# A gated linear recurrence and a maxout layer on one core: stores, tiled TensorE work and the order of the weight loads

## The chip, the cores and the metric

The kernel runs on one core of a Trainium2 chip. The core has five engines with queues of their own: TensorE (PE, with its weight loads shown as PEld), VectorE (DVE), ScalarE (ACT), GpSimd (POOL) and SyncE (SP). SP issues all transfers between device memory and the on-chip memory here. The metric is the device time of one execution in microseconds (us); the figure given is the median of five runs.

## What is computed

The input is a gated linear recurrence over 768 steps for 4 batches and 8 heads of width 48, followed by a layer with two weight matrices, a maximum and an output matrix:

```python
for t in range(S):
    state = alpha[:, :, t, :, None] * state + einsum('bhd,bhe->bhde', k[:, :, t], v[:, :, t])
    y[:, :, t] = einsum('bhd,bhde->bhe', q[:, :, t], state)
x = y.transpose(0, 2, 1, 3).reshape(3072, 384)
h1 = x @ w1                      # 384 x 1024
h2 = x @ w2
out = maximum(h1, h2) @ w_out    # 1024 x 384
```

All inputs and the output are float32. The kernel multiplies in float16.

## The kernel before

The sequence is cut into 24 chunks of 128 steps, six per batch. The first six (batch 0) are worked as three "doubles" of 256 steps (`m` = 0, 1, 2), the other eighteen (`n` = 6 to 23) one by one. For a chunk, the logarithms of alpha are summed by a matmul (`p1`, tile `cs`; in a double `dcs`), exponentials of the sums scale k and q (`kt`, `qt`), both are transposed on TensorE (`p2`, tile `tp`; `dtp`), the scores are made (`p3`, tiles `pa` and `pb`; `dp`), DVE masks them into `pt` (two steps, `m0` and `m1`), and `p4` (tile `y`; `dy`) adds the scores' product with v and the carried state's share. ACT copies `y` into the columns of `xT` (`a3`). The state `w` passes from chunk to chunk through `kv`, `t32` and `T`.

The maximum is rewritten: max(h1, h2) = relu(x(w1 - w2)) + x w2. So `wd` holds w1 - w2 (made by DVE in two halves), `m16` holds w2 w_out (384 x 384, made once on TensorE: `prep_m`, in two halves `i` for each of three row groups `s`), and the output is relu(x wd) w_out + x m. Chunks that are ready are taken in blocks of up to three (384 columns): eight steps `fstep` (tile `h`), each followed by a relu into `g`, and then for each chunk `tstep` in two halves (tile `op`: three matmuls with `m`, three and five with `w_out`), an eviction into a buffer `outs` and a store.

The order of all this is not written out by hand. A small planner (`Sched`) runs when the program is built. Each `Op` has a guess of its duration on each engine that may do it (`engs`), operations it must wait for (`deps`), operations that must be planned ahead of it (`after`), on-chip buffers it takes and reads (`Ring`, `Buf`) and a priority. `pick` looks at all operations of an engine, computes the earliest start of each, and takes the one with the smallest pair (start, priority); the engine whose choice starts first is advanced. What is planned becomes the fixed order of each engine's queue; on the chip every instruction waits for its real inputs, and those behind it wait with it. A matmul that uses only part of the array (`p3`, `p4` and the doubles' like) is marked `tiled`; a tiled operation gets 0.5 off its priority while the planner's TensorE is in the tiled state, and a change of state is charged 0.09 us. The matmuls of the second layer have priorities of 1000 and more, and so fill what attention leaves. `refill` adds a block of them when few are pending, a block of fewer than three chunks only if TensorE would be idle.

PSUM is shared by three rings: `rx` (3 buffers) for `cs`, `tp`, `kv` and the like; `rp` (2) for `pa` and `pb`; `rm` (3) for `y`, `h`, `op` and the accumulators of `m`. The accumulator of one `s` is taken by its first half and given back after the copy that follows its second.

SP's queue holds, in the planned order, the loads of the first double in parts, the six halves of the weights, the loads of the other doubles, and then four loads per chunk (alpha, k, q, v) with the stores of finished chunks among them. The float32 weights lie in `w1f`, `w2f` and `wof`; once they are converted to float16 (`prep_wd`, `prep_w2`, the `woc` copies), their space is used for the chunks' loads. The order of the weight loads is the line

```python
for x in "d0 w20 w21 wo0 w10 wo1 w11 d1 d2".split():
```

where `d0` to `d2` are the doubles. There are `NO` = 4 buffers for `outs`; a store is an operation of SP with a priority of -1 that depends on its eviction.

Of the kernel before, what the change touches and what calls it, by code (L numbers as in the profile page):

```python
# [15 lines left out]
class Op:  # L16


    def __init__(self, sched, name, n, engs, fn, deps=(), lat=0.1, alloc=(), reads=(), prio=0.0, tiled=False, after=()):
        self.name, self.n, self.engs, self.fn, self.lat = name, n, engs, fn, lat  # L20
        self.deps, self.alloc, self.prio, self.tiled = [d for d in deps if d is not None], list(alloc), prio, tiled
        self.after = [d for d in after if d is not None]
        self.done = None
        for b in list(alloc) + list(reads):
            b.users.append(self)
        for e in engs:
            sched.todo[e].append(self)
# [22 lines left out]
class Sched:  # L50


    SEM = 0.06
    MARGIN = 0.25

    def __init__(self):
        self.todo = {e: [] for e in ("PE", "ACT", "DVE", "POOL", "SP")}
# [28 lines left out]
    def pick(self, e):  # L86
        now = self.free[e]
        best = None
        for op in self.todo[e]:
            t = self.start(op)  # L90
            if t is None:
                continue
            margin = self.MARGIN if e == "PE" and op.prio < 1000 else 0.0
            late = max(t + margin, now)
            key = (late, op.prio - (0.5 if op.tiled and self.tiled else 0.0))
            if best is None or key < best[0]:
                best = (key, max(t, now), op)
        return best

    def run(self):  # L100
# [37 lines left out]
def kernel(  # L138
# [23 lines left out]
    C = 128  # L162
    NCH = S // C
    NCG = B * NCH
# [151 lines left out]
    st = {n: {} for n in range(NCG)}  # L316
# [250 lines left out]
    def more(m, u):  # L567
        return u == 0 or m < ND - 1
# [85 lines left out]
    def copy(e, out, in_):  # L654
        {"ACT": nc.scalar.copy, "DVE": nc.vector.tensor_copy, "POOL": nc.gpsimd.tensor_copy}[e](out=out, in_=in_)  # L655
# [16 lines left out]
    def prep_te(e, f):  # L672
        copy(e, w2T[:, f : f + 2, :].rearrange("p i m -> p (i m)"),
             st["w2", f][:, 0:6, :].rearrange("p i m -> p (i m)"))
# [45 lines left out]
    def store(t0):  # L720
        nc.sync.dma_start(out=out[t0 : t0 + C, :], in_=outs[t0])


    NG, NO = 3, 4
    S = Sched()
    rx, rp, rm = Ring(3), Ring(2), Ring(3)
    rl = [Ring(6) for _ in range(4)]
# [5 lines left out]
    def op(*a, **k):  # L733
        return Op(S, *a, **k)
# [19 lines left out]
    prev = None  # L754
# [10 lines left out]
                    GD[m]["ld", i, x] = prev  # L765

    lw2, lw1, lwo = [None] * 2, [None] * 2, [None] * 2
    for x in "d0 w20 w21 wo0 w10 wo1 w11 d1 d2".split():
        if x[0] == "d":
            dloads_of(int(x[1]), 0.3 * int(x[1]))  # L770
        else:
            i = int(x[2])
            fn, to = {"w2": (load_w2, lw2), "wo": (load_wo, lwo), "w1": (load_w1, lw1)}[x[:2]]
            prev = to[i] = op(x, i, {"SP": WLOAD / 2}, lambda e, i=i, fn=fn: fn(i), lat=1.6, after=[prev], prio=0.5)
# [3 lines left out]
            for s, c in enumerate(({"ACT": 0.54}, {"DVE": 0.4}, {"POOL": 0.8}))] for i in range(2)]  # L778
    wdc = [[op("wd", i, {"DVE": 1.7}, lambda e, i=i: prep_wd(i), deps=[lw1[i], lw2[i]], prio=0.2)] for i in range(2)]
    woc = [op("woc", f, {"ACT": 0.75, "DVE": 0.55},  # L780
              lambda e, f=f: copy(e, wo16[:, f : f + 2, :], wof[:, f : f + 2, :]), deps=[lwo[f // 4]], prio=-0.3)
           for f in range(0, NF, 2)]
# [8 lines left out]
    w2t = []  # L791
    for f in range(0, NF, 2):
        b = Buf(rx)
        t = op("w2t", f, {"PE": 0.4}, lambda e, f=f: prep_t(f), lat=0.17, deps=w2c[f // NFH], alloc=[b], prio=f - 10)
        w2t.append(op("w2te", f, {"DVE": 0.6, "ACT": 0.75}, lambda e, f=f: prep_te(e, f), deps=[t], reads=[b], prio=-0.4))
    mdone = []
    for s in range(3):
        b = Buf(rm)
        prev = None
        for i in range(2):  # L800
            prev = op("m", s, {"PE": 0.66}, lambda e, s=s, i=i: prep_m(s, i), lat=0.17,
                      deps=w2t[2 * i : 2 * i + 2] + woc[2 * i : 2 * i + 2], after=[prev],
                      alloc=[b] if i == 0 else (), reads=[b] if i else (), prio=0.4 + 0.01 * s)
        mdone.append(op("mev", s, {"ACT": 0.4, "DVE": 0.45}, lambda e, s=s: copy(e, m16[:, s, :], mps[s]),
                        deps=[prev], reads=[b]))

# [10 lines left out]
    for m in range(ND):  # L817
        g = GD[m]
# [17 lines left out]
        for h in range(2):  # L836
# [3 lines left out]
                alloc=al("loga"), reads=[L[0]] + re("loga"))  # L840
            add("p1", h, {"PE": 0.5}, lambda e, m=m, h=h: dcs(m, h), [g["a1", h]], lat=0.17, alloc=[("cs", h)], reads=["loga"])
            add("en", h, {"ACT": 0.44}, lambda e, m=m, h=h: dexp(m, h, "en", -1.0), [g["p1", h]],
                alloc=al("en"), reads=[("cs", h)] + re("en"))
            add("ep", h, {"ACT": 0.44}, lambda e, m=m, h=h: dexp(m, h, "ep", 1.0), [g["p1", h]],
                alloc=al("ep"), reads=[("cs", h)] + re("ep"))
            add("gg", h, {"ACT": 0.2}, lambda e, m=m, h=h: dgg(m, h), [g["p1", h]],
                alloc=al("gg"), reads=[("cs", h)] + re("gg"))
            add("kt", h, {"POOL": 1.05}, lambda e, m=m, h=h: dqk(m, h, 1), [g["en", h], g["ld", 1, h]],
                alloc=al("kt"), reads=["en", L[1]] + re("kt"))
            add("qt", h, {"DVE": 0.9}, lambda e, m=m, h=h: dqk(m, h, 2), [g["ep", h], g["ld", 2, h]],  # L850
                alloc=al("qt"), reads=["ep", L[2]] + re("qt"))
            add("v", h, {"POOL": 0.95} if m else {"POOL": 0.95, "ACT": 0.6}, lambda e, m=m, h=h: dv(e, m, h), [g["ld", 3, h], sdv[m % 2]],
                alloc=al("v"), reads=[L[3]] + re("v"))
            add("p2", h, {"PE": 0.44}, lambda e, m=m, h=h: dtp(m, h), [g["qt", h], g["kt", h]], lat=0.17,
                alloc=[("tp", h)], reads=["qt", "kt"])
            add("v2", h, {"DVE": 0.66, "ACT": 0.95}, lambda e, m=m, h=h: dtpe(e, m, h), [g["p2", h]],
                alloc=[("qk", h)], reads=[("tp", h)])
            add("p3", h, {"PE": 0.36}, lambda e, m=m, h=h: dp(m, h), [g["v2", h]], lat=0.17,
                alloc=[("pa", h), ("pb", h)], reads=[("qk", h)], tiled=True)
            for t in range(2):  # L860
                add("m" + str(t), h, {"DVE": 0.66}, lambda e, m=m, h=h, t=t: dmask(m, h, t),
                    [g["p3", h], smask, g.get(("m0", h))],
                    alloc=[] if t else [("pt", h)], reads=[(("pa", "pb")[t], h)] + ([("pt", h)] if t else []))
        add("pk", 0, {"PE": 0.38}, lambda e, m=m: dkv(m), [g["kt", 1], g["v", 1]], lat=0.17,
            alloc=[("kv", u) for u in range(2) if more(m, u)], reads=["kt", "v"], tiled=True)
        for u in range(2):
            m1, u1 = dbefore(m, u)
            if m1 >= 0:
                Bp, gp = B2[m1], GD[m1]
                add("g", u, {"POOL": 0.25}, lambda e, m=m, u=u: dg(m, u), [gp["gg", 1], g["gg", 1]],  # L870
                    alloc=[("g", u)], reads=[Bp["gg"], "gg"])
                if more(m, u):
                    add("t32", u, {"POOL": 0.56}, lambda e, m=m, u=u: dt32(m, u), [g["g", u], gp["w", u1]],
                        alloc=[("t32", u)], reads=[("g", u), Bp["w", u1]])
                first = u == 0 or m == 0
                for t in range(2):
                    add(f"T{t}", u, {"POOL": 0.56}, lambda e, m=m, u=u, t=t: dT(m, u, t),
                        [g["g", u], gp["w", u1], sdv[m % 2], g.get(("T0", u)) if t else None],
                        alloc=["T"] if first and t == 0 else (),
                        reads=[("g", u), Bp["w", u1]] + ([] if first and t == 0 else ["T"]))  # L880
            if more(m, u):
                add("w", u, {"DVE": 0.35}, lambda e, m=m, u=u: dw(m, u), [g["pk", 0], g.get(("t32", u))],
                    alloc=[("w", u)], reads=[("kv", u)] + ([("t32", u)] if m1 >= 0 else []))
        add("p4", 0, {"PE": 1.1 if m else 0.85}, lambda e, m=m: dy(m), [g["m1", 1], g["v", 1], g["T1", 1]], lat=0.17,
            alloc=[("y", 0), ("y", 1)], reads=[("pt", 0), ("pt", 1), ("qk", 0), ("qk", 1), "v", "T"], tiled=True)
        for u in range(2):
            G[2 * m + u]["a3"] = add("a3", u, {"ACT": 0.5}, lambda e, m=m, u=u: dx(m, u), [g["p4", 0]], reads=[("y", u)])

# [2 lines left out]
    for n in range(2 * ND, NCG):  # L891
        c = n % NCH
        g = G[n]
# [27 lines left out]
        if c:  # L921
            pg = G[n - 1]
            add("g", {"POOL": 0.25}, lambda e, n=n: vg(n), [pg["gg"], g["gg"]], alloc=["g"], reads=[B_[n - 1]["gg"], "gg"])
            if c < NCH - 1:
                add("t32", {"POOL": 0.56}, lambda e, n=n: vt32(n), [g["g"], pg["w"]], alloc=["t32"],
                    reads=["g", B_[n - 1]["w"]])
            for t in range(2):
                add(f"T{t}", {"POOL": 0.56}, lambda e, n=n, t=t: vT(n, t), [g["g"], pg["w"]],
                    alloc=["T"] if t == 0 else (), reads=["g", B_[n - 1]["w"]] + (["T"] if t else []))
                if t:  # L930
                    g["T1"].after.append(g["T0"])
        if c < NCH - 1:
            add("kv", {"PE": 0.18}, lambda e, n=n: p3k(n), [g["kt"], g["v1"]], lat=0.17, alloc=["kv"], reads=["kt", "v"])
            add("w", {"DVE": 0.75}, lambda e, n=n: vw(n), [g["kv"], g.get("t32")], alloc=["w"],
                reads=["kv"] + (["t32"] if c else []))
        add("p4", {"PE": 0.42 if c else 0.25}, lambda e, n=n: p4(n), [g["m1"], g["v1"], g.get("T1")], lat=0.17,
            alloc=["y"], reads=["pt", "v", "qk"] + (["T"] if c else []), tiled=True)
# [6 lines left out]
    def refill(now, idle):  # L944
        while pend and pend[0].done is not None:
            pend.pop(0)
        if len([o for o in pend if o.done is None]) > 2 or nxt[0] >= NCG:
            return
        if wdc[0][0].done is None or wdc[0][0].done > now + 0.3:
            return  # L950
        a = nxt[0]
        k = 0
        while k < WMAX // C and a + k < NCG and G[a + k]["a3"].done is not None and G[a + k]["a3"].done <= now + 0.3:
            k += 1
        if k == 0 or (k < WMAX // C and not idle):
            return
        nxt[0] += k
        W, a0 = k * C, a * C
        bg = Buf(rg16)
        rel = []  # L960
        xs = [G[a + i]["a3"] for i in range(k)]
        for f in range(NF):
            bh = Buf(rm)
            o = op("f", a, {"PE": 3 * max(W / 2400 + 0.0025, 0.07)}, lambda e, a0=a0, W=W, f=f: fstep(a0, W, f),
                   lat=0.17, deps=xs + wdc[f // NFH], after=pend[-1:], alloc=[bh] + ([bg] if f == 0 else []), prio=1000 + a)
            pend.append(o)
            rel.append(op("relu", a, {"ACT": 0.08 + W / 1200, "DVE": 0.1 + W / 960},
                          lambda e, a0=a0, W=W, f=f: relu(e, a0, W, f), deps=[o], reads=[bh, bg], prio=n))
        for i in range(k):
            bo, bs = Buf(rm), Buf(ro)  # L970
            for half in range(2):
                o = op("t", a + i, {"PE": (0.98, 0.82)[half]}, lambda e, a0=a0, i=i, half=half: tstep(a0, i, half),
                       lat=0.17, deps=mdone + woc + (rel[:3] if half == 0 else rel), after=pend[-1:],
                       alloc=[bo] if half == 0 else (), reads=[bg] if half else [bg], prio=1000 + a)
                pend.append(o)
            ev = op("oev", a + i, {"ACT": 0.4, "DVE": 0.45}, lambda e, t=a0 + i * C: oevict(e, t), deps=[o],
                    alloc=[bs], reads=[bo], prio=n)
            op("st", a + i, {"SP": 0.55}, lambda e, t=a0 + i * C: store(t), lat=1.2, deps=[ev], reads=[bs], prio=-1)
        return True

    S.refill = refill
# [32 lines left out]
```

## Time and profile before

| what | us |
|---|---|
| five runs | 149.21, 147.67, 147.69, 148.96, 151.07 |
| their median | 148.96 |
| the profiled execution | 148.49 |
| its span, first to last instruction | 146.7 |
| TensorE's first matmul | 4.01 |
| transposes of the second double begin | 28.29 |
| last matmul begins to drain; last eviction starts | 143.24; 143.32 |

Busy time of the engines in stretches of the span (us; DMA is the mean busy share of the 16 DMA engines, and can pass 1 where transfers overlap an edge of the stretch):

| stretch | PE | DVE | ACT | POOL | DMA |
|---|---|---|---|---|---|
| 0 to 12 | 5.03 | 5.86 | 4.86 | 9.42 | 0.88 |
| 12 to 19.5 | 4.96 | 6.37 | 5.05 | 4.23 | 1.06 |
| 19.5 to 28.3 | 6.34 | 3.70 | 6.20 | 1.95 | 1.07 |
| 28.3 to 45 | 16.70 | 12.92 | 12.30 | 14.17 | 0.98 |
| 45 to 60 | 14.49 | 9.73 | 11.82 | 11.19 | 0.99 |
| 60 to 90 | 30.00 | 20.03 | 24.10 | 19.33 | 0.96 |
| 90 to 118 | 28.00 | 19.77 | 21.48 | 18.82 | 0.99 |
| 118 to 143.3 | 25.24 | 4.56 | 14.47 | 3.01 | 0.20 |

A busy TensorE is not one at its peak: the end of a matmul is modelled, so a small pause between two matmuls can be hidden in "busy". Such pauses are read from the distance between two starts. The granted TensorE clock is 0.998 of full speed over the span.

### The profile page before, as it was taken

How to read it: one execution, taken by the hardware profiler on the slowest of the kernel's cores; microseconds unless marked ns; L12 is line 12 of the kernel's file. 1: busy time of each engine (PE TensorE's matmuls, PEld its weight loads, DVE VectorE, ACT ScalarE, POOL GpSimd, SP SyncE). 2: the span in 40 equal slices, each digit the busy share in tenths (PEclk: the TensorE clock that was granted, in tenths of full speed). 3: DMA queues.
4: the chain of work that ended last, by engine and by line, in shares of the span. 5: the costliest groups of instructions: out<-in, count | busy, mean ns of one | idle time of the engine just before them, and what ended most of it. 6: DMA issues, size and time to landing. Idle time of an engine off the chain costs nothing.

```text
span 146.7 us, 4865 instructions
## 1 busy us (share of the span) xinstructions
PE 130.8 (89%) x1958; PEld 87.4 (60%) x1958; DVE 82.9 (57%) x161; ACT 100.8 (69%) x223; POOL 82.1 (56%) x184
## 2 busy tenths in 40 slices
PE   0375789599999998999999999999999999999990
PEld 0353646476877676666667666666666665656550
DVE  4647754578494793886457865587469693100000
ACT  4433876676787778778677976886778656925721
POOL 7987400768997869664188954848468871000000
PEclk9999999999999999999999999999999999999999
DMA  4999999999799899979999999989999951102012
GB/s 121 261 348 382 381 341 238 245 274 202 137 201 217 166 220 222 196 144 234 197 206 192 216 200 221 225 196 228 180 215 230 202 132 54 54 30 111 24 69 92
DMA packets 93542, 28.62 MB, mean 195 GB/s; under 512 B 87888, under 2 KB 91984, under 8 KB 93520
## 3 DMA queue, kind: packets, MB, share of 16 engines
q1 hardware_dynamic: 93520, 28.32, 81.8%
q8 instruction: 15, 0.25, 0.7%
q14 instruction: 7, 0.06, 0.1%
HBM read 23.59 MB, written 4.72 MB: 193 GB/s over the span
## 4 chain that ended last, share of the span: by engine, by line
PE 72%; SPq 12%; DMA 9%; ACT 2%; issue 1%; DVE 1%; POOL 1%; ACTq 0%; POOLq 0%; DVEq 0%
PE op L711 21%; PE h L694 20%; PE op L708 8%; SPq L203 7%; DMA dqf<-in_q_dram 6%; PE y L465 6%; SPq L223 4%; DMA w1f<-in_alpha_dram 3%; PE pa L406 3%; PE tp L388 3%; PE tp L390 2%; PE cs L330 2%; PE kv L417 2%; PE dtp L533 1%; SPq L233 1%
## 5 line engine op out<-in xcount | busy, mean ns | idle before, releaser
L711 PE MATMUL op<-wo,g 128*128 128x384 f16 x192 | 37.3, 326 | 0.0
L694 PE MATMUL h<-xT,wd 128*128 128x384 f16 (+1 forms) x216 | 36.6, 309 | 0.0
L701 ACT ACTIVATE g<-h 128x384 f16<-128x384 f32 (+1 forms) x53 | 23.7, 467 | 2.8 <-PE h L694 2.6
L694 PEld LDWEIGHTS <-wd 128*128 128x128 f16 x216 | 19.2, 98 | 9.2
L711 PEld LDWEIGHTS <-g 128*128 128x128 f16 x192 | 17.9, 98 | 11.3
L425 DVE TENSOR_TENSOR pt<-pa,u 128x512 f16<-128x512 f32 x18 | 12.4, 691 | 12.5 <-PE pb L406 6.9
L655 ACT COPY outs<-op 128x384 f32<-128x384 f32 x20 | 9.6, 479 | 14.0 <-PE op L711 14.0
L367 POOL TENSOR_TENSOR T<-w,g 48x192 f16<-48x192 f32 x30 | 15.6, 519 | 1.2
L655 ACT COPY qk<-tp 128x1024 f16<-128x1024 f16 x15 | 15.2, 1012 | 1.1 <-PE tp L390 1.0
L708 PE MATMUL op<-m,xT 128*128 128x384 f16 x72 | 15.6, 325 | 0.0
L425 DVE TENSOR_TENSOR pt<-pb,u 128x512 f16<-128x512 f32 x18 | 12.3, 683 | 0.1
L469 ACT CAST xT<-y 128x384 f16<-128x384 f32 x18 | 8.7, 484 | 4.6 <-PE y L465 4.3
L521 POOL TENSOR_TENSOR dkt<-dkf,den 128x384 f16<-128x384 f32 x6 | 6.2, 1048 | 9.6 <-ACT den L503 9.6
L352 POOL TENSOR_TENSOR kt<-wof,en 128x384 f16<-128x384 f32 x6 | 6.5, 1087 | 8.3 <-ACT en L340 7.9
L436 DVE TENSOR_TENSOR w<-kv,t 48x192 f32<-48x192 f32 x24 | 8.5, 353 | 3.8 <-PE kv L417 3.4
L340 ACT ACTIVATE en<-cs 128x384 f32<-128x384 f32 x18 | 9.0, 498 | 0.8 <-PE cs L334 0.8
L699 DVE TENSOR_SCALAR g<-h 128x256 f16<-128x256 f32 (+1 forms) x19 | 8.6, 475 | 1.6 <-PE h L694 1.5
L340 ACT ACTIVATE ep<-cs 128x384 f32<-128x384 f32 x18 | 9.0, 502 | 0.0
L465 PE MATMUL y<-pt,v 128*32 128x128 f16 x288 | 9.0, 220 | 0.0
L352 POOL TENSOR_TENSOR kt<-w1f,en 128x384 f16<-128x384 f32 x6 | 6.4, 1062 | 3.7 <-ACT en L340 1.8
L708 PEld LDWEIGHTS <-xT 128*128 128x128 f16 x72 | 6.4, 97 | 3.3
L352 POOL TENSOR_TENSOR kt<-w2f,en 128x384 f16<-128x384 f32 x6 | 6.0, 1001 | 3.7 <-ACT en L340 3.3
(121 smaller groups left out, 269.7 us busy)
## 6 DMA issues: line engine op xcount, KB each, us to landing
out_dram<-outs SPq DMA_DIRECT2D x24, 192.0 KB, 3.0
w2f<-in_moe_w_dram SPq DMA_DIRECT2D x2, 768.0 KB, 7.5
wof<-in_moe_w_out_dram SPq DMA_DIRECT2D x2, 768.0 KB, 10.6
w1f<-in_moe_w_dram SPq DMA_DIRECT2D x2, 768.0 KB, 11.9
dvf<-in_v_dram SPq DMA_DIRECT2D x3, 384.0 KB, 5.8
wof<-in_alpha_dram SPq DMA_DIRECT2D x6, 192.0 KB, 4.9
wof<-in_k_dram SPq DMA_DIRECT2D x6, 192.0 KB, 4.3
wof<-in_q_dram SPq DMA_DIRECT2D x6, 192.0 KB, 4.4
```

Of the source, the lines that this page charges most:

```text
L203: nc.sync.dma_start(out=dloads[m][i][:, hs], in_=src[0, hs, m * C2 : (m + 1) * C2, :].rearrange("h (p j) d -> p h (j d)", j=2),)
L340: nc.scalar.activation(out=t, in_=csv, func=ACTF.Exp, scale=scale)
L352: nc.gpsimd.tensor_mul(out=kts[n % NB][:, :, 0:D], in0=loads[n][1], in1=st[n]["en"])
L367: nc.gpsimd.tensor_mul(out=st[n]["T16"][ps, :, D * t : D * t + D], in0=st[n - 1]["w"][ps], in1=st[n]["g"][ps].unsqueeze(2).to_broadcast([D ...
L425: nc.vector.tensor_mul(out=s["pt"][:, t], in0=s["pp"][t], in1=ub)
L465: nc.tensor.matmul(y[o : o + 32, b // 4, :], lhsT=lhsT, rhs=rhs, start=start, stop=stop)
L469: nc.scalar.copy(out=xT[:, :, n * C : (n + 1) * C], in_=st[n]["y"])
L655: {"ACT": nc.scalar.copy, "DVE": nc.vector.tensor_copy, "POOL": nc.gpsimd.tensor_copy}[e](out=out, in_=in_)
L694: nc.tensor.matmul(h[:, 0:W], lhsT=wd16[:, s, f * 128 : (f + 1) * 128], rhs=xT[:, s, a : a + W], start=(s == 0), stop=(s == 2))
L701: nc.scalar.activation(out=gts[a][:, f, 0:W], in_=hs[a, f][:, 0:W], func=ACTF.Relu)
L708: nc.tensor.matmul(op, lhsT=xT[:, s, t0 : t0 + C], rhs=m16[:, s, :], start=(s == 0), stop=False)
L711: nc.tensor.matmul(op, lhsT=gts[a][:, f, i * C : (i + 1) * C], rhs=wo16[:, f, :], start=False, stop=(f == NF - 1))
```

## The change

There are four edits in the planner and its input; no instruction of the computation is added or removed.

- Stores: an `Op` can have a `slack`, which is added to its earliest start when SP chooses and when it is planned. All stores but those of the last four chunks get 3.0 us. `NO` goes from 4 to 6.
- Tiled work: `pick` counts the tiled operations that can start within 0.1 us. On TensorE, outside the tiled state and after 45 us of the plan, if fewer than two are ready, a tiled operation that has been ready for less than `HOLD` = 2.5 us gets 2000 added to its priority, so that ready full-array work goes first. Within the tiled state a tiled operation now gets 2.0 off, not 0.5.
- Weight loads: w1's second half is loaded before w_out's second half.
- `prep_m`: the first half of each accumulator must be planned after `p4` of the first double.

```diff
+    HOLD = 2.5
...
     def pick(self, e):
         now = self.free[e]
         best = None
-        for op in self.todo[e]:
-            t = self.start(op)
+        ready = [(op, self.start(op)) for op in self.todo[e]]
+
+        hold = e == "PE" and not self.tiled and sum(op.tiled for op, t in ready if t is not None and t <= now + 0.1) < 2
+        for op, t in ready:
             if t is None:
                 continue
             margin = self.MARGIN if e == "PE" and op.prio < 1000 else 0.0
-            late = max(t + margin, now)
-            key = (late, op.prio - (0.5 if op.tiled and self.tiled else 0.0))
+            late = max(t + margin + op.slack, now)
+            prio = op.prio
+            if op.tiled and self.tiled:
+                prio -= 2.0
+            elif op.tiled and hold and now - t < self.HOLD and now > 45.0:
+                prio += 2000.0
+            key = (late, prio)
             if best is None or key < best[0]:
-                best = (key, max(t, now), op)
+                best = (key, max(t + op.slack, now), op)
         return best
...
-    NG, NO = 3, 4
+    NG, NO = 3, 6
...
-    for x in "d0 w20 w21 wo0 w10 wo1 w11 d1 d2".split():
+    for x in "d0 w20 w21 wo0 w10 w11 wo1 d1 d2".split():
...
-    mdone = []
+    mdone, mfirst = [], []
     for s in range(3):
         b = Buf(rm)
         prev = None
         for i in range(2):
             prev = op("m", s, {"PE": 0.66}, lambda e, s=s, i=i: prep_m(s, i), lat=0.17,
-                      deps=w2t[2 * i : 2 * i + 2] + woc[2 * i : 2 * i + 2], after=[prev],
+                      deps=w2t[2 * i : 2 * i + 2] + woc[2 * i : 2 * i + 2], after=[prev] if i else [],
                       alloc=[b] if i == 0 else (), reads=[b] if i else (), prio=0.4 + 0.01 * s)
+            if i == 0:
+                mfirst.append(prev)
...
+        if m == 0:
+            for o in mfirst:
+                o.after.append(g["p4", 0])
...
-            op("st", a + i, {"SP": 0.55}, lambda e, t=a0 + i * C: store(t), lat=1.2, deps=[ev], reads=[bs], prio=-1)
+            op("st", a + i, {"SP": 0.55}, lambda e, t=a0 + i * C: store(t), lat=1.2, deps=[ev], reads=[bs], prio=-1, slack=3.0 if a + i < NCG - 4 else 0.0)
```

More of the change, by code (lines that the diff above doesn't have):

```diff
@@ L16, with __init__ @@
 class Op:
-    def __init__(self, sched, name, n, engs, fn, deps=(), lat=0.1, alloc=(), reads=(), prio=0.0, tiled=False, after=()):
+    def __init__(self, sched, name, n, engs, fn, deps=(), lat=0.1, alloc=(), reads=(), prio=0.0, tiled=False, after=(), slack=0.0):
         self.name, self.n, self.engs, self.fn, self.lat = name, n, engs, fn, lat
@@ L22, in __init__ @@
         self.after = [d for d in after if d is not None]
-        self.done = None
+        self.done, self.slack = None, slack
         for b in list(alloc) + list(reads):
```

## The prediction

> **What bounds the kernel now.** I read the page first: busy shares by engine, the slices, the chain that ended last. Then TensorE's waits in two stretches, its timeline around the places that the diff touches, and the busy time by stage.
>
> The page's lines (columns: busy us, share of the span, instructions; then tenths busy in 40 slices of 3.67 us; then the chain's shares by engine):
>
> ```profile
> PE 130.8 (89%) x1958; PEld 87.4 (60%) x1958; DVE 82.9 (57%) x161; ACT 100.8 (69%) x223; POOL 82.1 (56%) x184
> ...
> PE   0375789599999998999999999999999999999990
> ...
> DMA  4999999999799899979999999989999951102012
> ...
> PE 72%; SPq 12%; DMA 9%; ACT 2%; issue 1%; DVE 1%; POOL 1%; ACTq 0%; POOLq 0%; DVEq 0%
> ```
>
> PE is full from the eighth slice to the end, the DMA engines are full up to about 118 us. The waits of PE, first for 0 to 28.3 us, then for 28.3 to 143.3 us, say which of the two sets the end (columns: who waited for whom, us in total, times, longest):
>
> ```profile
> PE dcs L488 <- ACT dloga L478: 6.2, 3, 4.0
> PE dtp L533 <- DVE dqt L519: 1.7, 1, 1.7
> PE dpa L550 <- ACT dqk L655: 1.5, 1, 1.5
> PE wtp L669 <- DVE dw L591: 1.1, 1, 1.1
> PE dpa L550 <- DVE dqk L655: 0.8, 1, 0.8
> PE mp L683 <- ACT wo L655: 0.6, 1, 0.6
> ```
> ```profile
> PE dtp L533 <- DVE dqt L519: 1.7, 1, 1.7
> PE cs L330 <- ACT loga L325: 0.5, 1, 0.5
> ```
>
> After 28.29 us, in 115 us, PE waits once, for 0.5 us (the 1.7 us ends at 28.29). So the kernel is a head of 28.3 us in which loads and short dependences rule, 115 us of PE work without holes, and a tail of 3.4 us (last eviction and store). The time changes if the head gets shorter, if PE does more before 28.29, if its work takes fewer us, or if holes open.
>
> The head's end, from the PE timeline (start, us, engine, line, operation, count, idle before):
>
> ```profile
> 19.52 0.90 PE L683 MATMUL mp<-wo,w2T 128*128 128x384 f16 x4
> 21.02 3.41 PE L683 MATMUL mp<-wo,w2T 128*128 128x384 f16 x20 [0.59 <-ACT wo L655]
> ...
> 25.48 1.14 PE L694 MATMUL h<-xT,wd 128*128 128x256 f16 x9
> 28.29 0.40 PE L533 MATMUL dtp<-ident,dqt 128*128 128x128 f16 x4 [1.67 <-DVE dqt L519]
> ```
>
> The chain of waits shows what the dtp waits for:
>
> ```profile
> 18.28 8.86 DMA dqf<-in_q_dram
> ...
> 27.23 1.02 DVE dqt L519
> ...
> 28.29 0.62 PE dtp L533 x8
> ```
>
> The second double's q is issued at 18.28 and lands at 27.1, behind all six weight halves in one queue that is full.
>
> **Part 1: load order and m.** w1's second half and wo's second half (768 KB each) change places in SP's queue. From the DMA issues by window the fifth half (wo 1) is issued at 8.06 and lands 12.1 us later, at 20.2; the sixth (w1 1) at 9.45, 13.1 us later, at 22.5. So w1 1 will land at about 20.2 and wo 1 at 22.5. What is behind them, dq of the second double among it, has the same bytes ahead and keeps 27.1. Consequences, step by step:
> - The second subtraction for wd (DVE, 1.76 us) runs 20.2 to 22.0 instead of 22.6 to 24.3. Nobody waited for it; gain 0 by itself.
> - The conversion of wo 1 (ACT 0.83 us beside DVE 0.72 us or less) runs 22.5 to 23.3. The second halves of m (12 matmuls) cannot start before. The twelve of the first halves can: one s at 19.5, the other two when the copies of the first y free PSUM (ring of 3; about 20.3 and 20.8 by the 0.5 us copies). They are 4 x 0.165 us each, so PE is through with them at about 21.5 and waits 1.8 us, in place of 0.59 us. The second halves then run 23.3 to 25.3 against an end of 24.4 before. All three accumulators of the ring are held until then, so no h can fill that wait.
> - Behind the waiting m on PE: two dcs (0.86 us), nine h (1.0 us), then dtp. 25.3 + 0.86 + 1.0 = 27.2, still before 28.29: the 1.67 us hole there covers the 0.9 us lost. Without that cover it would cost 0.9 us. On ACT, den and dep of the second double start at about 25.8 and dep ends near 26.7, 0.5 us before q has landed; dkt on POOL (1.0 us) ends near 27.5, before its transposes at 28.5.
> - y of the first double before m: the trace has it there already (dy begins at 18.10, the first mp at 19.52). The new edge fixes that order. 0.
>
> Sum of part 1: 0; between -1.7 (the hole before 28.29 filled with h) and +0.7 us (every step 0.7 us later than I put it, cover spent).
>
> **Part 2: tiled work taken together.** A chunk has one p3 (8 matmuls, 48-row tiles) and one y (28 matmuls, 32-column tiles), between full-array work. The price of going in and out, from the PE timeline:
>
> ```profile
> 80.82 1.63 PE L694 MATMUL h<-xT,wd 128*128 128x384 f16 x9
> 82.38 0.23 PE L406 MATMUL pa<-qk 48*128 48x128 f16 x1
> ```
>
> Nine h take 1.56 us from first start to the p3, where nine h ahead of full-array work take 1.46 (77.88 to 79.34). The same 0.10 us shows as 0.58 against 0.49 for three h ahead of a y. The y at 93.41 is followed by cs 0.52 us later; the y at 62.53 is followed by a p3 0.51 us later. So a p3 put straight behind a y saves its entry, 0.10 us, and nothing of y's way out.
>
> The Trainium skill, page "TensorEngine Tiling (Array Packing)", section Tiling Modes (Key Properties), says that a change of tiling mode drains the array. y and p3 are different modes, so by that rule alone a pair drains between its two members and after them, as often as two single groups do less one: the rule speaks against most of the gain. The rows say that the drain after y is indeed there in the pair (0.51 to 0.52 us either way) but that the entry cost on the full-array side is saved. By the rule read strictly part 2 is worth 0, by the rows 0.10 us a pair. I take the rows.
>
> Pairs: between 45 us and the end I count 18 p3, 18 y and one dy in 30 groups, so seven pairs stand already. If each chunk made one group, 19 would remain, 11 x 0.10 = 1.1 us. The hold lasts 2.5 us at most and drops when no full-array work is ready, so I take eight new pairs: -0.8 us. Bounds 0 and -1.1; two y side by side (same mode, some 0.25 us each with the way out) could add a little, the scores of two chunks cannot stand together since pa and pb fill their ring of two.
>
> What the hold delays: a held p3 delays its two masks (DVE 0.69 + 0.68 us), and they free pa and pb for the next chunk's p3; a held y delays the xT copy (ACT 0.48 us) and the h of its block. Full-array work runs meanwhile. Cover: the last y ends at 129.42 and the last block's h starts at 133.82, so 3.9 us remain after the copy; at 58.4 to 63.4 us (third y of the first single block to its h) 4.5 us. Below these the delay costs 0, above one for one.
>
> **Part 3: stores with slack, six output buffers.** Twenty of 24 stores move back by 3 us in the plan, past the loads behind them. Between 38 and 117 us SP waited 13 us in store instructions (sum of its rows). But PE's only wait on a load in that time is the 0.5 us at 55.4:
>
> ```profile
> PE cs L330 <- ACT loga L325: 0.5, 1, 0.5
> ```
>
> It hangs on a load issued at 49.89 and landed 4.84 us later; two stores (1.56 and 0.64 us of issue at 40.2 and 42.3) stand ahead of it. With them behind, the hole may close: 0 to -0.5, I take -0.3. POOL's queue issues no DMA. Two more buffers keep evictions from waiting for the later stores: three outputs come 1.8 us apart at the fastest, then a pause; a store needs 0.48 + 3 + 3.6 us. The last four stores keep no slack, so the tail of 3.4 us stays.
>
> **Sum.** 0 - 0.8 - 0.3 = -1.1 us on the profiled execution's 148.49 us (146.7 span, 1.8 around it): 147.4. The median of the five runs is 148.96, 0.47 above that execution, so 147.9 us on the scale of the runs. About 1% (1.5 us) is what a measurement of this kernel tells from no change.
>
> **The rivals.**
> - *The head is used* (0.15). With wd complete at 22.0 and DVE free, more h go into PE's queue ahead of dtp, and the 1.67 us hole fills: five more steps of three 256-wide h at 0.33 us. Against it: the ring of three held by m, and relu on an ACT busy with den and dep. 147.9 - 1.5 = 146.4 us.
> - *The hold stretches the attention chain, slower than before* (0.25). p3 of a chunk needs pa and pb back from the chunk before, so a hold is passed from chunk to chunk. Place: 45 to 129 us. Price: each us by which the last y comes after about 133.3 us. It decides from 3.9 us in all, 0.22 us per chunk over 18. With 0.35 us per chunk the last y is 6.3 us later, 2.4 us past its cover, plus a like hole where the early stock of h and op is thin (near 55 us, where the one wait stands), less the 0.8 gained: about 151.0 us. For it: a tiled step may be held 2.5 us, ten times that mean. Against: a hold only lets ready work go first, and PE's total is unchanged.
> - *It does nothing* (0.14). Drains as the page has them, or few new pairs; the hole at 55 us moves: 148.9 us.
>
> The likeliest (0.46) is the sum, 146.9 to 148.7. Faster by over 1% (under 147.5): four tenths of that, 0.18, and the first rival, 0.15, and 0.01 of the third: 0.34. Slower by over 1% (over 150.4): 0.24 from the second. Within 1%: 0.42. The range goes from 146.0 to 150.4 us: it leaves out the stretched chain's larger part (0.16) and a full head with all pairs (0.04).
>
> **What would show it.** Part 1: mp in two runs of twelve, with a wait of about 1.8 us for wo, dtp still near 28.3. Part 2: some 22 tiled groups after 45 us, and TensorE from dtp to its last op shorter by about 1 us. Part 3: stores after loads in SP's list, no wait of cs for loga. I am wrong if dtp moves by over 0.7 us either way, if waits of PE after 28.3 us sum to over 1.5 us, or if the blocks of h have other widths than six of 384 and three of 256.

## The result, and the profile after

| | before | changed |
|---|---|---|
| median of all runs, us | 149.05 (79 runs) | 148.97 (44 runs) |
| lowest, us | 147.52 | 146.82 |
| ratio | | 0.997, 95% interval 0.9948 to 0.9992 |
| profiled execution, us (span) | 148.49 (146.7) | 149.74 (148.0) |

The change takes 0.3% off, some 0.4 us, where 1.1 us was forecast. The ratio compares the faster executions of the two kernels alone, since some executions of either are a per cent or more slower, and both profiled executions of the changed kernel (149.74 us here, 149.02 in run e5) are among the slower ones, so their holes are read beside those of e6, which has the same order on TensorE from 46 to 57 us and whose profile (148.03 us) is not. I read the trace for where the time goes, and the ratio for how much it is.

The page of the changed kernel, the lines that answer to those of before:

```profile
PE 130.4 (88%) x1958; PEld 88.6 (60%) x1958; DVE 87.4 (59%) x163; ACT 99.2 (67%) x221; POOL 83.1 (56%) x184
...
PE   0474896899999697999999999999999999999990
...
DMA  4999999999989597989998999999989742010212
```

A new dip stands in PE's row at the 14th to 16th slice (48 to 59 us), where before has nines and one 8, and the DMA row dips in the same slices. PE's waits from 28.3 us to the end say the same:

```profile
PE cs L338 <- ACT loga L333: 1.8, 2, 1.4
PE h L702 <- ACT xT L477: 0.5, 1, 0.5
PE tp L396 <- ACT qk L663: 0.2, 1, 0.2
```

Before had one wait of 0.5 us there. The changed kernel's sum to 2.57 us. What was gained is visible too. In the PE timeline of the changed kernel a chunk's y is followed by the next chunk's p3 and only then by full-array work (a few of the rows):

```profile
82.02 0.24 PE L342 MATMUL cs<-gcol,loga 128*128 128x2 f16 x4
82.19 0.24 PE L473 MATMUL y<-qk,T 112*32 112x128 f16 x4
...
82.71 0.23 PE L414 MATMUL pa<-qk 48*128 48x128 f16 x1
...
83.04 0.50 PE L702 MATMUL h<-xT,wd 128*128 128x384 f16 x2
```

Counted over the whole timeline from 45 us on, the 37 tiled steps stand in 19 groups; they stood in 30. And the head, from the same view:

```profile
19.49 2.52 PE L691 MATMUL mp<-wo,w2T 128*128 128x384 f16 x12
23.31 2.11 PE L691 MATMUL mp<-wo,w2T 128*128 128x384 f16 x12 [1.31 <-ACT wo L663]
...
26.12 1.14 PE L702 MATMUL h<-xT,wd 128*128 128x256 f16 x9
27.97 0.40 PE L541 MATMUL dtp<-ident,dqt 128*128 128x128 f16 x4 [0.70 <-DVE dqt L527]
```

The first and second halves of m are parted by a wait for wo, as worked out, and dtp begins at 27.97 (28.29 before).

How the largest hole is made is in PE's order. First the changed kernel, then the one before, at the same work (some rows of each):

```profile
49.59 0.82 PE L702 MATMUL h<-xT,wd 128*128 128x256 f16 x6
51.78 0.32 PE L338 MATMUL cs<-loga,cmat 128*128 128x384 f16 x1 [1.37 <-ACT loga L333]
51.94 0.24 PE L342 MATMUL cs<-gcol,loga 128*128 128x2 f16 x4
52.11 0.23 PE L414 MATMUL pa<-qk 48*128 48x128 f16 x1
...
52.44 0.41 PE L473 MATMUL y<-pt,v 128*32 128x128 f16 x16
```
```profile
50.25 0.49 PE L694 MATMUL h<-xT,wd 128*128 128x256 f16 x3
50.68 0.23 PE L406 MATMUL pa<-qk 48*128 48x128 f16 x1
...
51.28 0.41 PE L465 MATMUL y<-pt,v 128*32 128x128 f16 x16
...
52.08 0.33 PE L330 MATMUL cs<-loga,cmat 128*128 128x384 f16 x1
```

Before, p3, kv, y and tp stand ahead of the sums of chunk 9. The hold pushes p3 and y behind them, and the queue is in order: when chunk 9's alpha is late, p3 waits with it. The load of that alpha was not issued late: at 45.63, where before issued it at 45.87. It landed 5.5 us after its issue, against 4.1 us before, and behind it SP stood 2.81 us in the issue of the next load (SP's list of the changed kernel: start, us):

```profile
43.33 1.07 SPq L729 DMA_DIRECT2D out_dram<-outs  x1
44.44 0.43 SPq L202 DMA_DIRECT2D w2f<-in_v_dram  x1
44.97 0.62 SPq L729 DMA_DIRECT2D out_dram<-outs  x1
45.63 0.44 SPq L202 DMA_DIRECT2D w2f<-in_alpha_dram  x1
46.17 2.81 SPq L202 DMA_DIRECT2D w2f<-in_k_dram  x1
```

Two stores, moved back by the slack, now stand right ahead of it; before they stood ahead of chunk 8's alpha and k (40.17 and 42.31). That alone does not make it late: in the seven profiles of other kernels with the two stores in this place (e2, e4, e6, e7, e14 to e16) it landed after 4.0 to 5.1 us, and in the nine without them after 4.1 to 4.8. In e5 it took 5.8.

The wait of h for xT is a wait for a buffer, not for its numbers. This h is the last of the eight steps of the block of chunks 4 and 5, and the other seven had run. But h and y take their PSUM from one ring of three, and a buffer came free only when ACT had copied the y of chunk 7. ACT, in order too, stood at the logarithm of chunk 10's alpha, with that copy behind it (three rows of ACT, then PE's):

```profile
56.70 0.52 ACT L333 ACTIVATE loga<-w1f 128x384 f16<-128x384 f32 x1 [1.37 <-DMA w1f<-in_alpha_dram]
57.13 0.99 ACT L663 COPY qk<-tp 128x1024 f16<-128x1024 f16 x1
58.03 0.48 ACT L477 CAST xT<-y 128x384 f16<-128x384 f32 x1
```
```profile
58.56 0.49 PE L702 MATMUL h<-xT,wd 128*128 128x256 f16 x3 [0.53 <-ACT xT L477]
```

### The profile page after: what moved, and what is told of

It reads as the page before. It is cut to its first block, busy times and chain, and to the rows that moved or that the text cites. A ratio compares the mean times of both kernels' runs of the same rounds, so it can differ in the third digit from the quotient of the medians.

```text
span 148.0 us, 4866 instructions
## 1 busy us (share of the span) xinstructions
PE 130.4 (88%) x1958; PEld 88.6 (60%) x1958; DVE 87.4 (59%) x163; ACT 99.2 (67%) x221; POOL 83.1 (56%) x184
## 3 DMA queue, kind: packets, MB, share of 16 engines
q1 hardware_dynamic: 93520, 28.32, 80.3%
## 4 chain that ended last, share of the span: by engine, by line
PE 72%; DMA 12%; SPq 7%; ACT 3%; issue 2%; DVE 1%; POOL 1%; ACTq 0%
PE op L719 21%; PE h L702 20%; DMA wof<-in_moe_w_out_dram 8%; PE op L716 8%; PE y L473 5%; DMA w1f<-in_alpha_dram 4%; PE pa L414 3%; SPq L231 3%; SPq L211 2%; PE tp L396 2%; PE tp L398 2%; PE cs L338 2%; SPq L202 1%; PE kv L425 1%; PE mp L691 1%
## 5 line engine op out<-in xcount | busy, mean ns | idle before, releaser
L719 PE MATMUL op<-wo,g 128*128 128x384 f16 x192 | 36.8, 326 | 0.0
L663 ACT COPY outs<-op 128x384 f32<-128x384 f32 x21 | 10.1, 480 | 16.5 <-PE op L719 16.5
L663 ACT COPY qk<-tp 128x1024 f16<-128x1024 f16 x14 | 14.2, 1017 | 2.3 <-PE tp L398 2.2
L375 POOL TENSOR_TENSOR T<-w,g 48x192 f16<-48x192 f32 x30 | 15.1, 503 | 1.1
```

The lines of the kernel that those rows point to most:

```text
L375: nc.gpsimd.tensor_mul(out=st[n]["T16"][ps, :, D * t : D * t + D], in0=st[n - 1]["w"][ps], in1=st[n]["g"][ps].unsqueeze(2).to_broadcast([D ...
L719: nc.tensor.matmul(op, lhsT=gts[a][:, f, i * C : (i + 1) * C], rhs=wo16[:, f, :], start=False, stop=(f == NF - 1))
```

## The experiments

For the profiles I compare the stretch from the second double's dtp to the start of the last op group, PE's idle in it, and the number of tiled groups after 45 us, counted in the timeline. "Net" is the stretch less the idle. "Hole" is PE's idle from 45 to 60 us.

| kernel | groups | dtp | stretch | idle | net | hole | ratio (interval) |
|---|---|---|---|---|---|---|---|
| before | 30 | 28.29 | 109.43 | 0.51 | 108.92 | 0.51 | 1 |
| changed | 19 | 27.97 | 110.99 | 2.57 | 108.42 | 2.57 | 0.997 (0.9948-0.9992) |
| e5, changed again | 19 | 27.85 | 110.39 | 1.99 | 108.40 | 1.99 | 0.9963 (0.9929-0.9997) |
| e1, pairs alone | 20 | 28.34 | 108.65 | 0.53 | 108.12 | 0.00 | 0.9959 (0.9922-0.9995) |
| e11, e1 again | 20 | 28.77 | 108.23 | 0.29 | 107.94 | 0.18 | |
| e2, slack alone | 31 | 28.38 | 109.98 | 0.79 | 109.19 | 0.72 | 0.9988 (0.9958-1.0018) |
| e3, loads and m alone | 30 | 28.32 | 110.03 | 1.06 | 108.97 | 0.69 | 1.0021 (0.9986-1.0057) |
| e13, changed without slack | 20 | 28.40 | 109.55 | 1.11 | 108.44 | 0.38 | 0.999 (0.996-1.002) |
| e6, changed with old loads | 19 | 27.77 | 109.49 | 1.07 | 108.42 | 1.07 | 0.9958 (0.9931-0.9985) |
| e15, e6 again | 19 | 28.54 | 109.45 | 1.02 | 108.43 | 1.02 | |
| e4, changed, hold from 60 | 22 | 30.82 | 107.86 | 0.00 | 107.86 | 0.00 | 0.9971 (0.9938-1.0004) |
| e14, e4 again | 22 | 28.27 | 108.91 | 0.81 | 108.10 | 0.81 | |
| e7, e4 with old loads | 22 | 28.13 | 107.85 | 0.00 | 107.85 | 0.00 | 0.994 (0.9915-0.9965) |
| e16, e7 again | 22 | 28.34 | 108.72 | 0.70 | 108.02 | 0.70 | 0.9923 (0.9895-0.995) |
| e8, pairs from 60 alone | 22 | 27.61 | 109.46 | 1.42 | 108.04 | 1.42 | 0.9932 (0.9905-0.9958) |
| e12, e8 again | 22 | 28.25 | 107.87 | 0.00 | 107.87 | 0.00 | |
| e9, tiled steps apart | 37 | 28.32 | 109.92 | 0.34 | 109.58 | 0.34 | 1.0065 (1.0039-1.0091) |

### e1, e2, e3: one part alone

Each is the kernel before with one part of the change. The parts as diffs, shortened:

```diff
# e1
...
+            prio = op.prio
+            if op.tiled and self.tiled:
+                prio -= 2.0
+            elif op.tiled and hold and now - t < self.HOLD and now > 45.0:
+                prio += 2000.0
# e2
-    NG, NO = 3, 4
+    NG, NO = 3, 6
-            ... prio=-1)
+            ... prio=-1, slack=3.0 if a + i < NCG - 4 else 0.0)
# e3
-    for x in "d0 w20 w21 wo0 w10 wo1 w11 d1 d2".split():
+    for x in "d0 w20 w21 wo0 w10 w11 wo1 d1 d2".split():
...
+        if m == 0:
+            for o in mfirst:
+                o.after.append(g["p4", 0])
```

> The kernel before with the hold and the stronger pull of the tiled state alone; stores, buffers and load order as before. 20 tiled groups after the first p3 (30 before). Theory (the pairs save 0.10 us each, and the hold puts a cs whose alpha is late ahead of a ready p3 between 48 and 58 us): PE waits for loga there sum to 1 to 2.5 us, the ten pairs give back 1.0, ratio 0.995 to 1.008. Rival (the holes come from the moved stores and loads): no wait above 0.6 us after 28.3, ratio 0.992 to 0.994. Second rival (a change of tiling mode drains, so pairs save nothing): with the holes, ratio 1.005 to 1.015.

> The kernel before with the slack of the stores and six output buffers alone. 31 tiled groups. Theory: the order on PE up to 62 us is that of before, the one wait of cs stays between 0 and 0.6 us, ratio 0.997 to 1.002. Rival (moved stores make the holes): PE waits after 28.3 sum to over 1.5 us, ratio 1.006 to 1.015.

> The kernel before with w1's second half loaded ahead of w_out's second half, and m after the first double's y, alone. 30 tiled groups. Theory: mp waits 1.0 to 1.9 us for wo, dtp of the second double starts at 28.0 to 28.5 as before, ratio 0.997 to 1.003. Rival (the late m moves dtp): dtp at 28.8 or later, ratio over 1.003. Rival (the holes after 45 us come from this part): PE waits after 28.3 sum to over 1.5 us.

Pairs alone: 0.9959, with 20 groups and none of the large holes: in its trace PE waits for loga only 0.2 us after dtp. Of the two readings that I had put up, the ratio fits the first (0.995 to 1.008) and the waits fit its rival, so the early hold alone is not what makes the holes. Slack alone: 0.9988, nothing that can be measured. Loads and m alone: 1.0021, with dtp where it was (28.32) and mp waiting 1.7 us. In these profiles no single part makes a hole of 1 us or more.

### e4, e14, e7: the hold from 60 us on, with the new and the old load order

```diff
-            elif op.tiled and hold and now - t < self.HOLD and now > 45.0:
+            elif op.tiled and hold and now - t < self.HOLD and now > 60.0:
```

e7 has the load order and the place of m of before besides.

> The changed kernel with the hold from 60 us of the plan on, not from 45: 22 tiled groups, and the order of TensorE up to about 62 us is that of before. Theory: the waits of PE between 45 and 60 us fall back to under 0.7 us, eight pairs stay at 0.10 us each, ratio to before 0.990 to 0.996. Rival (pairs save nothing): ratio 0.998 to 1.002. Rival (the holes come from stores or loads): waits of 1.5 to 2.5 us between 45 and 60 us as in the changed kernel, ratio about 1.00 or more.

> Run e4 once more. If the late head belongs to the program: mp waits about 3 us for wo, a slice of PEclk near 22 us at half, dtp of the second double after 30 us. If it is chance of the execution: mp waits 1.3 to 2 us, PEclk full, dtp at 27.8 to 28.4.

In e4's profile the waits between 45 and 60 us are gone and the stretch is 1.57 us shorter than before's, yet the ratio of its executions is 0.9971 and not 0.990 to 0.996. What the profile lost, it lost in the head: dtp begins at 30.82. The PE timeline of e4:

```profile
19.43 2.24 PE L691 MATMUL mp<-wo,w2T 128*128 128x384 f16 x12
24.80 3.17 PE L691 MATMUL mp<-wo,w2T 128*128 128x384 f16 x12 [3.13 <-ACT wo L663]
...
29.23 1.14 PE L702 MATMUL h<-xT,wd 128*128 128x256 f16 x9
30.82 0.34 PE L541 MATMUL dtp<-ident,dqt 128*128 128x128 f16 x3 [0.45 <-DVE dqt L527]
```

wo 1 was converted from 23.91 on, 1.5 us later than in the changed kernel's profile, so PE waited 3.13 us. Then the twelve second-half matmuls took 3.0 us from their first start to the dcs, against 1.95 (23.31 to 25.26) there. The page of e4 shows why, in the row of the granted clock:

```profile
PEclk9999999599999999999999999999999999999999
```

One slice, the eighth, 25.8 to 29.5 us, was granted half speed; in steps of 1 us the clock is 0.84 from 25 to 26, 0.50 to 29 and 0.95 to 30. The Trainium skill says in "TensorE: Matmul & The Clock Gate", in the table of "Why this matters for your kernels", that an idle gap of about 3 us between bursts puts the array back to half rate. Here half speed followed a wait of 3.13 us once, some 0.9 us after the wait had ended, and did not follow waits of 1.3 to 1.8 us for the same copy (changed kernel, e3, e5, e13, e14). e14, the same kernel, has mp waiting 1.5 us, a full clock and dtp at 28.27: e4's late head is chance of the execution, as that expectation put it for the second case. Nor does the new load order meet a low clock more often: a mean granted clock of 0.99 or less, as in e4's profile (0.988), is on record in 13 of 125 executions of the kernels with the new order and in 31 of 345 of those with the old one. Why the ratio of all of e4's executions missed its range stays open.

> The changed kernel with the old load order and the hold from 60 us on: 22 groups. Theory: no wait over 0.7 us after the second double's dtp, 1.3 to 1.6 us less from that dtp to the last op than before, head as before, ratio 0.988 to 0.993: the fastest. Rival (the head's chain is not what the fourth run lost): as that run, 0.996 to 0.998.

e7 keeps the hold from 60 us and goes back to the old load order. Its only wait of PE after 28 us is the end of the head's hole:

```profile
PE dtp L541 <- DVE dqt L527: 1.7, 1, 1.7
```

The ratio is 0.994, just outside what was expected (0.988 to 0.993).

### e5, e6: the changed kernel again, and with the old load order

e6 puts back the loads' order and m's place, nothing else (the diff of e3 reversed).

> The changed kernel, unchanged, executed again: one more profile of it. Theory: PE waits for loga between 45 and 60 us again, 1 to 2.5 us in all, mp waits 1 to 3 us for wo; 19 groups; ratio 0.995 to 1.002. Rival (the holes of the first profile were chance of that execution): waits after 28.3 under 0.6 us, ratio 0.992 or less.

> The changed kernel with the load order and the place of m as before: pairs and slack stay, 19 groups. Theory (with wo last, its landing, the end of m, dcs and dep stand in one chain ahead of dtp, and late executions pass on in full): ratio 0.991 to 0.997, below the changed kernel's 0.997; mp waits under 1 us. Rival (the load order is neutral): ratio equal to the changed kernel's in this call within 0.002.

e5's waits for loga sum to 1.3 us, and those for xT and qk are again 0.5 and 0.2: the hole repeats, 1.99 us of idle. e6 has 0.3 us of waits for loga and the same 0.5 and 0.2. So the 0.7 us comes in each of these profiles, and the wait at chunk 9's sums varies with the landing of its alpha. In the ratio the two are alike (0.9963 and 0.9958): the old load order earned no more than its rival allowed.

### e8: the late hold alone

> The kernel before with the hold from 60 us on and nothing else: stores without slack, four output buffers, old load order; 22 groups. Theory: eight pairs at 0.10 us, the one wait of cs at 55 us stays at about 0.5 us; ratio 0.990 to 0.996. If the slack of the stores is worth something beside the pairs, this is 0.002 or more above the run with slack in the same call.

Stores and loads as before, the hold from 60 us on: 0.9932. It is not 0.002 above e7's 0.994 but level with it: no worth of the slack shows beside the pairs either. Its hole of 1.42 us was larger than expected, with TensorE's order there that of before.

### e9: tiled steps kept apart

```diff
-            key = (late, op.prio - (0.5 if op.tiled and self.tiled else 0.0))
+            key = (late, op.prio + (2000.0 if op.tiled and self.tiled else 0.0))
```

> The kernel before, with the planner's sign turned round: in the tiled state a tiled step gives way to any ready full-array work, so no two tiled steps are neighbours: 36 groups where before has 30. Theory (0.10 us for every entry, whatever tiled step came before): the stretch from the second double's dtp to the last op, less PE's waits, is 0.5 to 0.7 us longer than before's; ratio 1.003 to 1.006. Rival (a change of mode drains in a pair as well, so pairs are worth nothing): stretch less waits within 0.2 us of before's, ratio 0.998 to 1.002.

Seven groups more than before cost 0.66 us net (109.58 against 108.92), 0.09 us each, and the ratio is 1.0065: pairs are worth what the rows said. In the table net falls from 109.58 (37 groups) over 108.92 and 108.97 (30) to 107.85 to 108.10 (22), 0.10 to 0.12 us a group. Below 22 groups no more gain shows: with 20 it is 107.94 and 108.12 in the two profiles with the smallest holes (e11, e1) and 108.44 in e13, and with 19 it is 108.40 to 108.43, 0.6 us above what eleven entries at 0.10 us would make of 108.92. I take most of the 0.6 us for a hidden part of the holes: the end of a matmul is modelled (a row of 0.33 us that the next may follow after 0.16), so a hole's first 0.16 us counts as busy, and these kernels have two or three holes more than before. That is an estimate, of 0.3 to 0.5 us.

### e10: the second double's loads ahead of w_out

On e7, the loads in the order below, and m taken as a whole once w_out is converted (shortened):

```diff
-    for x in "d0 w20 w21 wo0 w10 wo1 w11 d1 d2".split():
+    for x in "d0 w20 w21 w10 w11 d1 wo0 wo1 d2".split():
-                      deps=w2t[2 * i : 2 * i + 2] + woc[2 * i : 2 * i + 2], ...
+                      deps=w2t[2 * i : 2 * i + 2] + woc, ...
```

> Run e7 with the loads of the second double ahead of both halves of w_out, and m as a whole after both are converted. Theory (the head ends when q of the second double has landed, and m only has to come before the first op): dtp of the second double at 25 to 26.5 us in place of 28.1, more h done ahead of it, no hold of PSUM by m; ratio 0.980 to 0.990. Rival (the head is set by the sum of the loads, and what comes earlier for dtp comes later for m and op): PE waits for wo appear at 28 to 31 us in place of the others, ratio as e7, 0.992 to 0.996.

A miss: 1.0269 (1.0218 to 1.0321). dtp did begin at 24.38, but m came at 27.68 with two waits for wo:

```profile
27.68 0.81 PE L691 MATMUL mp<-wo,w2T 128*128 128x384 f16 x4 [0.64 <-ACT wo L663]
29.92 3.41 PE L691 MATMUL mp<-wo,w2T 128*128 128x384 f16 x20 [1.43 <-ACT wo L663]
```

Ready work behind m, the doubles' dp among it, stood until 33.26. And the blocks changed: seven of 384 columns and three of 128, where before had six of 384 and three of 256; one block of 128 is the last of all, at 141.97. I take what the head won to be lost to the order that the planner made of it; no run separates the two.

### e11, e12, e13, e15, e16: what repeats

> Run e1 once more, for a second profile of the early hold without slack. If holes at 45 to 60 us belong to the program: PE busy 14.8 to 15.0 us of that stretch again. If they are chance of the execution: anything from 12.4 to 15.0.

> Run e8 once more, for a second profile of the late hold without slack. If holes belong to the program: PE busy about 13.6 us of 45 to 60 again. If chance: anything from 13.5 to 15.0.

> The changed kernel without the slack and with four output buffers: new load order, m after y, hold from 45 us; 20 groups. Theory (the holes need slack and early hold together): PE busy 14.5 us or more of 45 to 60; mp still waits 1.3 us or more for wo. Rival (new load order and early hold make the holes): PE busy under 13.5 us there. Ratio 0.994 to 1.000 by the theory, 0.998 to 1.004 by the rival.

> Run e6 once more (slack and early hold, old load order). If slack and early hold together make the holes: PE busy 13.0 to 14.3 us of 45 to 60. If they are chance: 14.5 or more.

> Run e7 once more (old load order, slack, hold from 60 us), for a second comparison with the kernel before: ratio 0.991 to 0.997, stretch from dtp to the last op 107.8 to 108.5 us, PE busy 14.5 us or more of 45 to 60.

e13 is the changed kernel with slack 0.0 and four buffers. With the early hold and without slack the hole is 0.00, 0.18 and 0.38 us (e1, e11, e13); with both it is 2.57, 1.99, 1.07 and 1.02 (changed, e5, e6, e15); with the order of before up to 60 us, slack or not, it is 0.00 to 1.42 (nine profiles, mean 0.54), and e8 and e12, one kernel, have 1.42 and 0.00. So large holes are in part chance, and in all four profiles that join slack and early hold they are at least 1.0 us, of which 0.7 (h for xT, tp for qk) is the same each time; the 0.2 of tp is in e11 and e13 too, the 0.5 of h in none of the three.

All seven profiles with the early hold have one order on PE from 46 to 57 us, and differ there in when the loads land: chunk 10's alpha landed 3.8 to 4.4 us after its issue in the three without slack and 5.1 to 5.6 us in the four with it, and e1 has ACT at its logarithm at 53.79 without a wait and no wait of h. That the large hole needs order and slack together is what four profiles against three suggest; e8's 1.42 us, with neither, shows how far one profile can be trusted. Dropping the slack did not make the whole measurably faster: e13's ratio is 0.999 (0.996 to 1.002), and its PE waits between 60 and 90 us instead (29.26 busy of 30).

e16 is e7 once more and comes to 0.9923 (0.9895 to 0.995). Old loads with the hold from 60 us is below before in both its comparisons and lies about 0.4% below the changed kernel's ratio on record; where e7 was timed beside the changed kernel (e5), the intervals overlap (0.9915 to 0.9965 and 0.9929 to 0.9997).

## Why the prediction was wrong

It had the direction and one of three sizes. The forecast was 1.1 us, in place of which 0.4 came. One of its own signs of being wrong came up too: PE's waits after 28.3 us sum to 2.57 us, where it allowed 1.5.

**Part 2, pairs: size right.** "eight new pairs: -0.8 us", with a bound of 1.1. All eleven formed. The 0.10 us per entry holds in e9 (0.09 us for each group more) and in the runs with 22 groups: eight pairs with the order of before up to 60 us give ratios of 0.994, 0.9932 and 0.9923 (e7, e8, e16), 0.9 to 1.1 us. So the choice between row and rule holds: y and p3 are different modes, and the pair still saves the entry.

**The step that failed** is the sentence on the hold, "Cover: the last y ends at 129.42 and the last block's h starts at 133.82 ... Below these the delay costs 0". It asked only which later steps need the held step's results. It left out two things. One is what takes the held step's place at the head of PE's queue: the planner put there the sums of chunk 9, which it thought ready, and their alpha was not. Before, p3, kv, y and tp (1.4 us) stood ahead of them and covered that. The other is what a held y keeps: its PSUM buffer, which the next h needed while ACT stood at a late alpha. In the changed kernel's profile the cost is 1.8 us of waits for loga and 0.7 us of waits for buffers (the xT and qk copies); in e6 it is 0.3 and the same 0.7.

**Part 3, slack: sign wrong.** "I take -0.3", the hole at 55 us closing. It opened: 0.51 became 2.57 and 1.99 us, and 1.07 and 1.02 with the old load order (e6, e15). The forecast took the stores at 40.17 and 42.31 to get behind the load issued at 49.89. With 3 us more they stand at 43.33 and 44.97, still ahead of that load (now at 50.98) and closer to chunk 9's alpha. Alone the slack shows no effect, 0.9988 with an interval over 1; with the early hold it goes with the holes.

The two terms are about what is missing. A hole that closed by 0.3 us was forecast, and in e6 and e15 it grew by 0.5 to 0.6, some 0.8 us between forecast and outcome; the forecast of the whole was missed by 0.7. In e6 the stretch after dtp is 109.49 us against 109.43, so gain and holes cancel there. How the loss divides among early hold, slack and load order in the times is not shown: e1 (0.9959), e6 (0.9958) and e13 (0.999) have overlapping intervals.

**Part 1, head: 0, near the mark in the profile, but one reserve that it counted on was not there.** m waited 1.31 us (1.8 worked out), its second halves ran 23.31 to 25.26, dtp came at 27.97. "dep ends near 26.7, 0.5 us before q has landed" was no reserve: dep ended at 26.74, q had landed 8.3 us after its issue at 18.37, so by 26.7, and dqt started at 26.77, released by dep. wo, m, dcs, dep and dqt had become one chain, and a late wo passes through it, as in e4. The kernels with the new order were slower than the like ones with the old: e3 against before 0.0021, e13 against e1 0.0031, e4 against e7 0.0031, e5 against e6 0.0005. No one of these pairs is apart by its intervals, so a cost of about 0.3 us for this part is possible and not shown.

**The rivals.** The stretched chain did not decide: the last y came at 132.74 in place of 128.90, but the last block's h began at 135.06, and PE was busy between. That rival had named the place of the hole, "near 55 us", and expected it with the loss of the cover at the end, which did not come. The used head did not come: nine h before dtp, as before. The rule read strictly, as rival, is refuted by e9.

The sum on the profiled execution: dtp 0.3 us earlier, eleven entries 1.1 us less, holes 2.1 us more by the busy time and about 0.5 more by their modelled ends, +1.2 us in all; measured 149.74 against 148.49, +1.25. The 0.5 is the estimate of above, for three holes more. By the ratio the holes must be smaller in most executions than in the two profiles of this kernel; e6 and e15 have 1.0 us, and how large they are on average, no run here shows.

**Left open.** Why some loads land late, and why SP sticks in a load at 46 to 47 us while the DMA engines run empty. One load's issue takes 2.45 to 2.87 us in six of the profiles with slack (changed, e2, e5, e6, e14, e15) and 1.40 to 2.32 in the four others; without slack it takes 1.53 to 2.00, in before 1.63. The DMA share of the changed kernel from 48.5 to 49.5 us was 0.13. SP's wait list puts 2.4 us of SP's 2.81 down to POOL's kt of chunk 8, which ends at 48.58; but in e1 and e7 the like issue (48.61, 47.79) is over before that kt is (48.96, 48.74), so it does not need it. An instruction fetch of 16 KB on another queue falls between 46 and 48 us in all of them, and in before too; I did not separate it.

## What to carry to other kernels

When a step is held back in an in-order queue, cost what comes to the head in its place, with the measured arrival of its data and not the planner's, and what buffer the held step keeps from others. A weight moved to the end of the load order must be checked for the chain that it heads and for how long its reader then idles. Pairing tiled steps was worth the entry here, 0.1 us each, and the pairs made after 60 us of the plan, where TensorE of the kernel before never waited, gave all of the gain that can be seen: start it there.

## What the runs showed of the hardware

- A p3 behind a y costs no entry though their tile shapes differ (0.51 to 0.52 us from y's start either way), and each entry from full-array work costs 0.09 to 0.12 us, from 37 groups down to 22.
- TensorE was granted half speed for 3.4 us once, from some 0.9 us after a wait of 3.13 us (e4), and not after waits of up to 1.8 us.
- The DMA engines can be nearly empty (a share of 0.13 for 1 us) while SP stands in the issue of a load, in a stretch where their share was 0.99 before the change.
- One load of 192 KB, chunk 9's alpha, landed 4.0 to 5.8 us after its issue with the same two stores right ahead of it.
